# Moving one attention product into the next unit's group, and two output projection chunks to later steps

## The chip, the cores and the metric

The kernel runs on one core of one Trainium2 chip. The metric is the device time of one execution in microseconds (us). Engines: TensorE (PE; its weight loads are PEld), VectorE (DVE), ScalarE (ACT), GpSimd (POOL) and SyncE (SP), which only issues transfers. Each engine works through its own instructions in order and waits on semaphores of the others. TensorE writes to PSUM, eight banks of 128 partitions by 512 floats; VectorE and ScalarE read them.

## The reference

One transformer block on 2048 tokens of width 576: a modulated layer norm, attention with 32 heads of width 18 in four segments of 512 tokens and a memory that goes from segment to segment, an output projection with a residual, a second modulated norm, and a gated MLP of width 4608. The part that matters here:

```python
for s in range(N):
    qs, ks, vs = q[:, :, s], k[:, :, s], v[:, :, s]
    logits = jnp.einsum("bhqd,bhkd->bhqk", qs, ks) * scale + mask
    p = _softmax(logits, axis=-1)
    a_dot = jnp.einsum("bhqk,bhkd->bhqd", p, vs)
    ...
    o = g * a_mem + (1.0 - g) * a_dot
...
return o @ wo
```

The mask subtracts 1e9 where the key index is below the query index, so a query sees its own key and the later ones. All is float32.

## The kernel before

The kernel has three stages. The first (to 244.9 us of the profile) makes the projections and memory states, and already begins the maxima of the first units. The second, from 244.9 to 599.9 us, is the attention, and the third is the rest of the output projection and the MLP. The change touches the second stage only.

**Units and steps.** The attention is cut into 32 units: segment `s` and a group `q` of four heads, `u = 8 s + q`. A loop (L1350 on) runs over `u` and one more round for what is left over, with 11 steps `k` in each unit. The order of the instructions is the order in which this loop calls functions; nothing else schedules them. Each step takes, in this order:

- one piece of `p2_step(u, j)` (L590): the logits of one key block `j` of 128 keys against the queries, transposed (keys on partitions). These are the score matmuls, L601, into one of two banks `s2`, and the exponential on ScalarE, L604, from there to `Pt`. Block 0 takes steps 0 to 3 (one head each, 512 queries), block 1 steps 4 to 7 (384 queries), block 2 steps 8 and 9 (two heads each, 256 queries), block 3 step 10 (four heads, 128 queries). Behind a block GpSimd masks it (L608). `Pt` has one buffer for each block.
- one piece of `p1_step(u + 2, ...)` (L172): the logits of a unit two ahead in the other orientation, only for the row maxima. These are the maximum matmuls, L182, into one of two banks `s1`, and the reduction with the mask on VectorE, L187. Steps 0 to 3 have one reduction of 512 keys each, steps 4 to 7 one of 384, steps 8 and 9 two of 256, step 10 four of 128. The reduction of step `k` empties the bank that the maximum matmul of step `k + 2` writes.
- the events that the table `PAT` (L60) lists for this step. It has four rows: even and odd units of the first half of a segment (`q` below 4), and even and odd units of the second half.

**The events that matter.** `V0` to `V3` (`av_step`, L612) multiply block `j` of `Pt` with the values: four matmuls for four heads, each on 32 columns of the array (L621), which run at the same time and add into one bank `av`. Before, `V0` and `V1` belong to the unit at hand and `V2` and `V3` to the one before. `E` copies `av` with ScalarE (L633), `m` transposes the maxima (L201), `c` and `d` transpose and normalize the result. `M0` to `M3` (`wo_m`, L731) are the four chunks of one half of a 128-token tile of the output projection, of 3, 4, 3 and 4 matmuls, in one bank `w`; `X` (`wo_x`, L736) adds them to the residual on VectorE, which frees the bank, and at every second unit stores the tile (L738). They run in units 9 to 32. `R`, `S`, `T`, `Z`, `z` prepare the projection's left operand (`T` is L715 on VectorE, `z` is L693), `P`, `Q`, `q`, `Y` its weights in units 0 to 5 (`Y` is `wol`, L914, on VectorE); `l`, `p`, `x` are the second norm, `f`, `g`, `h` the memory's feature map (`g` is three ScalarE instructions, L780 to L782), `A` to `D` and `G` the memory's part.

Of the kernel before, what the change touches and what calls it, by code (L numbers as in the profile page):

```python
# [15 lines left out]
P = 128  # L16
S = 2048
D = 576
# [38 lines left out]
NE = 2  # L57
E1 = 3
E2 = 2
PAT = (["", "M0", "V2 V3 m E D", "", "n M1 Q G", "c", "M2 d", "V0 g", "h A0 q M3 R S X", "T Y Z B0", "A1 P V1 z B1 f C"],  # L60
# [3 lines left out]
LNA = 1  # L64
S1B, S2B, XB, WB = 2, 2, 2, 1

# [6 lines left out]
def block(ctx: ExitStack, tc: tile.TileContext, x, wqk, wv, wo, beta, wgu, wd, c, w_mod, out):  # L73
# [8 lines left out]
    def chain(*g):  # L82
        for a in g:
            yield from a
# [113 lines left out]
    def mt_a(u, ps, tag, bufs):  # L198
        mc = mcol.pop(u)[1]
        pmt[u] = ps.tile([P, L], F32, tag=tag, name="pmt", bufs=bufs)  # L200
        nc.tensor.transpose(pmt[u][:32, :P], f32(mc).rearrange("p a b c -> p (a b c)"), ident)  # L201

    def mt_b(u):
        mrow[u] = mr = mwk.tile([32, P], F32, tag="mr", name="mr")
        nc.scalar.copy(mr, pmt.pop(u)[:32, :P])
        put_m(u, u % NB)
# [38 lines left out]
    with ExitStack() as p1:  # L245
# [78 lines left out]
        with ExitStack() as p0:  # L324
# [41 lines left out]
            for b in range(3):  # L366
                n = P if b < 2 else 64
# [89 lines left out]
        def proj(s, t):  # L457
            hh, hl, hr = hT[s]
            pp = ps.tile([P, L], F32, tag="p", name="pp", bufs=3)
            mm14(pp, lambda k: wqkh[:, t, k, :], lambda k: wqkl[:, t, k, :], lambda k: hh[k],  # L460
                 lambda k: hl[k], lambda: hr, True)
            f = pb.tile([P, L], F32, tag="pf", name="pf")
            fh = pb.tile([P, L], F32R, tag="fh", name="fh")
            fl = pb.tile([P, L], F32R, tag="fl", name="fl")
            nc.scalar.copy(fh, pp)
            nc.scalar.copy(f, pp)
            nc.vector.tensor_tensor(fl, f, f32(fh), op=ALU.subtract)
            k0, k1 = 128 * t, min(128 * t + 128, D)
            if k0 < D:
                n = k1 - k0  # L470
                nc.sync.dma_start(kD[s][k0:k1, 0:2, :], f32(fh[:n]).unsqueeze(1).to_broadcast([n, 2, L]))
                nc.sync.dma_start(kD[s][k0:k1, 2, :], f32(fl[:n]))
            q0, q1 = max(128 * t - D, 0), 128 * t + 128 - D
            if q1 > 0:
                n = q1 - q0
                r = P - n
                nc.sync.dma_start(qD[s][q0:q1, 0:3:2, :], f32(fh[r:]).unsqueeze(1).to_broadcast([n, 2, L]))
                nc.sync.dma_start(qD[s][q0:q1, 1, :], f32(fl[r:]))
                if s > 0:
                    nc.sync.dma_start(qF[s][q0:q1, :], f[r:])  # L480
            return f
# [34 lines left out]
        for s in range(NSEG):  # L516
# [5 lines left out]
            g = chain(*gens)  # L522
# [6 lines left out]
            for t in QKORD:  # L529
# [4 lines left out]
                f = proj(s, t)  # L534
# [77 lines left out]
    def av_step(u, j):  # L612
        if u < 0 or u >= NU:
            return
        s, q = units[u]
        if j == 0:
            av[u] = ps.tile([P, L], F32, tag="av", name="av", bufs=1)
        pt = Pt.pop((u, j))
        for h in range(4):
            hh = 4 * q + h  # L620
            nc.tensor.matmul(av[u][32 * h:32 * h + 32, 128 * j:L], lhsT=vq[s][:, j, VW * hh:VW * hh + 32],  # L621
                             rhs=pt[:, h, :L - 128 * j], start=(j == 0), stop=(j == 3))
# [3 lines left out]
    def ev_step(u):  # L626
        if u < 0:
            return
        t = wk.tile([P, L], F32, tag="avs", name="avs")
        if u < NE - 2:  # L630
            nc.vector.tensor_copy(t, av.pop(u))
        else:
            nc.scalar.copy(t, av.pop(u))  # L633
        avs[u] = t

    def comb_a(u):
        if u < 0:
            return
        t = avs[u]
        avs[u] = px = ps.tile([P, 4, P], F32, tag="x", name="px", bufs=XB)  # L640
        for i in range(4):
            nc.tensor.transpose(px[:, i, :], t[:, 128 * i:128 * i + 128], ident)  # L642
# [127 lines left out]
    def phi_q(s, t):  # L770
        r = 64 if t == 0 else 0
        q0 = 0 if t == 0 else 64 + 128 * (t - 1)
        f = wk.tile([P, L], F32, tag="qf", name="qf", bufs=2)
        nc.sync.dma_start(f[r:], qF[s][q0:q0 + P - r, :])
        return f

    def phi_q2(s, t, f):
        r = 64 if t == 0 else 0
        e = wk.tile([P, L], F32, tag="qe", name="qe", bufs=1)
        nc.scalar.activation(e[r:], f[r:], AF.Relu, scale=-1.0)  # L780
        nc.scalar.activation(e[r:], e[r:], AF.Exp, scale=-1.0)
        nc.scalar.activation(f[r:], f[r:], AF.Relu)  # L782
        return e
# [61 lines left out]
    def event(ev, u):  # L845
        n, a = ev[0], ev[1:]
        s, q = divmod(u, 8)
        if n == "V":
            j = int(a)
            av_step(u if j < 2 else u - 1, j)  # L850
        elif n == "E":
            ev_step(u - 1)
        elif n == "m":
            if NE <= u + 1 < NU:
                mt_a(u + 1, ps, "x", XB)
        elif n == "n":
            if NE <= u + 1 < NU:
                mt_b(u + 1)
        elif n == "c":
            comb_a(u - 1)  # L860
        elif n == "d":
            comb_b(u - 1)
        elif n == "f":
            sn, qn = divmod(u + 1, 8)
            if u + 1 < NU and sn < 3 and qn < 5:
                fq[u + 1] = phi_q(sn + 1, qn)
        elif n in "gh" and s < 3 and q < 5:
            if n == "g":
                fq[-2] = phi_q2(s + 1, q, fq[u])
            else:  # L870
                phi_q3(s + 1, q, fq.pop(u), fq[-2])
        elif n in "DG" and u > 0:
            s1, q1 = divmod(u - 1, 8)
            if s1 < 3 and q1 >= 4:
                (num_d if n == "D" else num_e)(s1 + 1, q1 - 4, fq[-3])
        elif n in "ABC" and s < 3 and 4 <= q < 8:
            if n == "A":
                num_a(s + 1, q - 4, int(a))
            elif n == "B":
                num_b(s + 1, q - 4, int(a))  # L880
            else:
                fq[-3] = num_c(s + 1, q - 4)
        elif n in "Zz" and 1 <= s < 4 and q == 0:
            (wo_z if n == "Z" else wo_z2)(s - 1)
        elif n in "RST" and 1 <= s < 4 and q % 2 == 0:
            (wo_r if n == "R" else wo_s if n == "S" else wo_t)(s - 1, q // 2)
        elif n in "MX":
            w = u - 9
            if w >= 0 and w < 24:
                si, h = divmod(w, 2)  # L890
                if n == "M":
                    wo_m(si // 4, si % 4, h, int(a))
                else:
                    wo_x(si // 4, si % 4, h)
        elif n in "lpx":
            w = (u - 9) | 1 if u % 2 == 0 else u - 10
            if 0 <= w < 23:
                if n == "l":
                    ln_a(w // 8, w % 8 // 2)
                elif n == "p":  # L900
                    ln_b()
                else:
                    ln_c()
        elif n == "P" and s == 0 and q < 5:
            fq[-1] = wk.tile([P, D], F32, tag="woraw", name="woraw", bufs=1)
            nc.sync.dma_start(fq[-1], wo[:, q, :])
        elif n in "QqY" and s == 0 and 1 <= q < 6:
            k = q - 1
            if n == "Q":
                nc.gpsimd.tensor_tensor(fq[-1], fq[-1], gaB, op=ALU.mult)  # L910
            elif n == "q":
                nc.scalar.copy(woh[:, k], fq[-1])
            else:
                nc.vector.tensor_tensor(wol[:, k], fq[-1], f32(woh[:, k]), op=ALU.subtract)  # L914
# [212 lines left out]
    O, W, R, RW, DP = {}, {}, {}, {}, {}  # L1127
# [79 lines left out]
    T, SG, AC, AP = {}, {}, {}, {}  # L1207
# [136 lines left out]
    with tc.manual_schedule():  # L1344
# [5 lines left out]
        for u in range(NU + 1):  # L1350
            s, q = divmod(u, 8)
# [3 lines left out]
            for k in range(11):  # L1355
# [4 lines left out]
                if u == 24 and k == 0:  # L1360
                    stage_b()
                for ev in PAT[q // 4 * 2 + u % 2][k].split():
                    event(ev, u)
# [37 lines left out]
        for i in range(4):  # L1401
            for h in range(2):
                for c in range(WC):
                    n = 8 * i + 4 * h + c
# [4 lines left out]
                    if n in SS:  # L1409
                        j = SS.index(n)  # L1410
# [3 lines left out]
                    if n in WW:  # L1414
                        j = WW.index(n)
# [21 lines left out]
        n, nw = 0, PF  # L1437
# [5 lines left out]
        for t in range(2):  # L1443
            for p in range(NPR):
# [16 lines left out]
                for k in range(14):  # L1461
                    z, m = ZM[k]
# [67 lines left out]
                    if prev is not None and is_plain(*prev):  # L1530
# [3 lines left out]
                        if CH0[t][k]:  # L1534
                            f = plain(*prev, chunk)
# [20 lines left out]
                    if is_plain(t, p):  # L1556
                        if k in DK[dl // 2]:
                            j = DK[dl // 2].index(k)
# [74 lines left out]
```

## Time and profile before

| what | us |
|---|---|
| median of three runs | 1890.95 (1889.97 to 1894.65) |
| the profiled execution | 1891.12 |
| its span, first to last instruction | 1889.4 |
| first stage | 0 to 244.9 |
| attention stage | 244.9 to 599.9 |
| last stage | 599.9 to 1889.4 |

The page gives each engine's busy time, the chain that ended last, and groups of instructions by line. A row of the windows gives a stretch, its length, and the busy time and the number of instructions of TensorE, its weight loads, VectorE, ScalarE and GpSimd, then the granted clock, the share of the DMA engines and their rate. A row of the waits says who waited for whom: total us, times, longest. A row of the timeline has start, duration, engine, line, operation, what is written and read, the shape, the number of instructions merged, and in brackets the idle time of the engine before it with the instruction that ended it. A busy TensorE is modelled: the difference of two starts is the better measure of what a matmul costs.

### The profile page before, as it was taken

To read this page: it belongs to the slowest core of one execution; us is meant where nothing else is said; L and a number is where in the kernel's file an instruction comes from. 1 tells how busy PE (TensorE), PEld (TensorE's weight loads), DVE (VectorE), ACT (ScalarE), POOL (GpSimd) and SP (SyncE) were. 2 spreads that over 40 slices of the span, in tenths; PEclk is the share of its full clock that TensorE was granted. 3 is DMA by queue.
4 is the path that set the end of the run, shared out by engine and by line. 5 is a ranking of instruction groups with operands and counts; after the bars stand their busy time and mean duration, and the time that the engine had idled before them with its cause. 6 is when DMAs were issued, how large, how long until landed. Compare 5 with 4: busy or idle time off the path is not lost.

```text
span 1889.4 us, 30685 instructions
## 1 busy us (share of the span) xinstructions
PE 1861.1 (98%) x10927; PEld 1564.1 (83%) x10927; DVE 1495.0 (79%) x3279; ACT 971.8 (51%) x2128; POOL 532.1 (28%) x713
## 2 busy tenths in 40 slices
PE   7999999999999999999999999999999999999999
PEld 5888866777766788888888888888888888888888
DVE  6556368888886888888888988867888888888887
ACT  4433477768676544544544454444454444444442
POOL 2000046555556354455455455300000000000000
PEclk9999999999999999999999999999999999999999
DMA  8767654447555845544554544487233332333331
GB/s 246 261 204 257 218 175 133 145 132 201 168 161 186 293 146 179 182 144 168 169 177 144 191 141 142 162 275 227 79 122 103 121 106 77 125 103 118 102 100 57
DMA packets 179424, 304.31 MB, mean 161 GB/s; under 512 B 26152, under 2 KB 107688, under 8 KB 177352
## 3 DMA queue, kind: packets, MB, share of 16 engines
q1 hardware_dynamic: 150696, 245.29, 41.6%
q10 hardware_dynamic: 28576, 57.07, 8.5%
q8 instruction: 86, 1.41, 0.3%
q14 instruction: 66, 0.54, 0.1%
HBM read 187.98 MB, written 113.77 MB: 160 GB/s over the span
## 4 chain that ended last, share of the span: by engine, by line
PE 91%; DVE 3%; ACT 2%; DMA 1%; POOL 1%; issue 1%; SPq 0%; ACTq 0%; DVEq 0%; POOLq 0%
PE A L1204 24%; PE pd L1325 13%; PE C L1204 12%; PE pd L1308 10%; PE B L1204 6%; PE pp L99 5%; PE s L601 4%; PE s L182 4%; PE av L621 4%; PE pv L99 3%; PE pw L731 3%; DVE junk L187 1%; PE pn L802 1%; PE pm L449 1%; PE px L642 1%
## 5 line engine op out<-in xcount | busy, mean ns | idle before, releaser
L1204 PE MATMUL A<-y,wh 128*128 128x512 f32 x1152 | 407.1, 394 | 2.8 <-ACT tc L1233 2.0
L187 DVE CUSTOM_DVE_ANT_0 junk<-s,tri 128x256 bf16<-128x256 f32 (+3 forms) x512 | 227.9, 487 | 65.9 <-PE s L182 58.8
L1169 DVE TENSOR_TENSOR wl<-O,wh 128x256 fp32r<-128x256 f32 x504 | 258.5, 518 | 2.3 <-ACT wh L1168 1.8
L1204 PEld LDWEIGHTS A<-y,wh 128*128 128x128 f32 x1152 | 217.1, 188 | 47.8 <-ACT tc L1233 2.4
L1204 PE MATMUL A<-y,wl 128*128 128x512 f32 x576 | 227.2, 394 | 0.0
L604 ACT ACTIVATE Pt<-s 128x512 f32<-128x512 f32 (+1 forms) x352 | 186.1, 559 | 53.6 <-PE s L601 48.1
L1313 DVE TENSOR_TENSOR acc<-acc,pd 128x576 f32<-128x576 f32 x216 | 162.4, 752 | 58.6 <-PE pd L1308 51.5
L1159 POOL TENSOR_TENSOR O<-O 128x384 f32<-128x384 f32 x140 | 160.0, 1156 | 164.9 <-DMA O<-in_wgu_dram 72.5
L1204 PE MATMUL C<-y,wh 128*128 128x512 f32 x576 | 202.7, 392 | 1.8 <-DVE cu L1227 1.8
L1168 ACT CAST wh<-O 128x256 fp32r<-128x256 f32 x504 | 197.7, 406 | 1.7 <-issue 0.9
L1325 PE MATMUL pd<-dh,ah 128*128 128x288 f32 x640 | 189.2, 296 | 0.0
L1325 PE MATMUL pd<-dh,al 128*128 128x288 f32 x640 | 189.1, 296 | 0.0
L1325 PE MATMUL pd<-dl,ah 128*128 128x288 f32 x640 | 188.9, 295 | 0.0
L1329 DVE TENSOR_TENSOR acc<-acc,pd 128x576 f32<-128x576 f32 x156 | 116.9, 750 | 89.2 <-PE pd L1325 89.1
L1268 ACT CAST ah<-sg 128x512 fp32r<-128x512 f32 x192 | 119.4, 622 | 81.9 <-DVE sg L1228 81.7
L601 PE MATMUL s<-qs,ks 110*128 110x512 f32 (+2 forms) x384 | 148.3, 403 | 2.9 <-ACT Pt L604 2.4
L1269 DVE TENSOR_TENSOR al<-sg,ah 128x512 fp32r<-128x512 f32 x192 | 135.3, 704 | 9.9 <-ACT ah L1268 9.7
L182 PE MATMUL s<-ks,qs 108*128 108x256 f32 (+3 forms) x512 | 142.0, 329 | 0.9 <-DVE mx L187 0.2
L1308 PE MATMUL pd<-dh,ah 128*128 128x288 f32 x448 | 133.0, 297 | 0.0
L1308 PE MATMUL pd<-dh,al 128*128 128x288 f32 x448 | 132.5, 296 | 0.0
L1308 PE MATMUL pd<-dl,ah 128*128 128x288 f32 x448 | 132.3, 295 | 0.0
L1204 PEld LDWEIGHTS C<-y,wh 128*128 128x128 f32 x576 | 108.3, 188 | 22.3 <-DVE cu L1227 2.2
(361 smaller groups left out, 4385.1 us busy)
## 6 DMA issues: line engine op xcount, KB each, us to landing
O<-in_wgu_dram SPq DMA_DIRECT2D x36, 768.0 KB
oD<-O ACTq DMA_DIRECT2D x36, 512.0 KB
O<-oD SPq DMA_DIRECT2D x36, 512.0 KB
ks<-kD SPq DMA_DIRECT2D x64, 216.0 KB
qs<-qD SPq DMA_DIRECT2D x64, 216.0 KB
O<-in_wgu_dram SPq DMA_DIRECT2D x36, 384.0 KB
rD<-wr ACTq DMA_DIRECT2D x36, 336.0 KB
wr<-rD SPq DMA_DIRECT2D x35, 336.0 KB
```

The costliest lines, as they stand in the source:

```text
L99: nc.tensor.matmul(ps, lhsT=a, rhs=b, start=(k == 0), stop=(k == 13))
L182: nc.tensor.matmul(bank[:, n * (h - h0):n * (h - h0) + n], lhsT=qst[b][0:108, h, 128 * i:128 * i + 128], rhs=kst[b][0:108, h // 2, 0:n], s ...
L187: nc.vector.tensor_tensor_reduce(junk[:, :n], bank[:, n * (h - h0):n * (h - h0) + n], tri[:, L - n:], 1.0, -3e38, op0=ALU.add, op1=ALU.max ...
L601: nc.tensor.matmul(bank[:, n * (g - h):n * (g - h + w)].rearrange("p (a b) -> p a b", a=w), lhsT=kst[u % NB][0:110, g // 2, 128 * j:128 * ...
L604: nc.scalar.activation(pt[:, h:h + per, :n], bank[:, :n * per].rearrange("p (a b) -> p a b", a=per), AF.Exp, scale=SCALE)
L1159: eng.tensor_tensor(o[:, d], o[:, a], o[:, b], op=op)
L1168: nc.scalar.copy(wh, o)
L1169: later.append(lambda: nc.vector.tensor_tensor(wl, o, f32(wh), op=ALU.subtract))
L1204: nc.tensor.matmul(bank, lhsT=a, rhs=b, start=(first and n == 0), stop=(n == 6), skip_group_check=not first)
L1308: nc.tensor.matmul(pd[:, i, :288], lhsT=a[:, tk], rhs=w, start=(k == 0), stop=(k == 2))
L1313: nc.vector.tensor_tensor(o, o, pd[:, :, :288], op=ALU.add)
L1325: nc.tensor.matmul(pd[:, i, :288], lhsT=a[:, tk], rhs=w, start=(k == 0), stop=(k == 5))
```

## The change

`V1` leaves step 10 and stands in front of `V2` and `V3` in the next unit, at step 2 (step 3 in the last row), and `av_step` is told that blocks 1 to 3 belong to the unit before. `M3` with `X` goes to step 9 from step 8 or 6; in the last row `X` stays in step 10 and `M3` comes to step 9 from step 6. In the first two rows `M2` goes from steps 6 and 4 to steps 8 and 6. Only the table and one line differ:

```diff
-PAT = (["", "M0", "V2 V3 m E D", "", "n M1 Q G", "c", "M2 d", "V0 g", "h A0 q M3 R S X", "T Y Z B0", "A1 P V1 z B1 f C"],
-       ["D", "l M0 Q", "V2 V3 m E", "M1", "G p n A0 B0 M2", "", "M3 X A1 q c x d B1", "f", "V0 g", "", "C V1 Y h P"],
-       ["", "M0", "V2 V3 m E", "", "D G M1 c n", "", "Q V0 d g R", "h", "M2 q M3 A0 S B0 X", "Z Y", "P f z V1 A1 T B1 C"],
-       ["", "M0", "l D p G", "V2 V3 m E", "n M1 M2 A0", "", "M3 x c", "B0", "V0 d Q", "A1 g", "q X V1 Y B1 h P C f"])
+PAT = (["", "M0", "V1 V2 V3 m E D", "", "n M1 Q G", "c", "d", "V0 g", "h A0 q M2 R S", "T Y Z B0 M3 X", "A1 P z B1 f C"],
+       ["D", "l M0 Q", "V1 V2 V3 m E", "M1", "G p n A0 B0", "", "M2 A1 q c x d B1", "f", "V0 g", "M3 X", "C Y h P"],
+       ["", "M0", "V1 V2 V3 m E", "", "D G M1 c n", "", "Q V0 d g R", "h", "M2 q A0 S B0", "Z Y M3 X", "P f z A1 T B1 C"],
+       ["", "M0", "l D p G", "V1 V2 V3 m E", "n M1 M2 A0", "", "x c", "B0", "V0 d Q", "A1 g M3", "q X Y B1 h P C f"])
...
         if n == "V":
             j = int(a)
-            av_step(u if j < 2 else u - 1, j)
+            av_step(u - (j > 0), j)
```

## Prediction

> **What bounds the kernel now.** I read the page first, then the busy time by stage, then the waits of the attention stage (244.9 to 599.9 us, the only one that the change touches), then its timeline at the ends of units.
>
> ```profile
> PE 1861.1 (98%) x10927; PEld 1564.1 (83%) x10927; DVE 1495.0 (79%) x3279; ACT 971.8 (51%) x2128; POOL 532.1 (28%) x713
> ...
> PE 91%; DVE 3%; ACT 2%; DMA 1%; POOL 1%; issue 1%; SPq 0%; ACTq 0%; DVEq 0%; POOLq 0%
> ```
>
> ```profile
> core 0: us, PE busy (x) PEld busy (x) DVE busy (x) ACT busy (x) POOL busy (x), PEclk, DMA share, GB/s
> ...
> 334.50:419.50 85.00, 84.95 (x652) 62.81 (x652) 68.92 (x290) 61.66 (x127) 44.48 (x93) 1.00 0.47 141
> ```
>
> ```profile
> DVE junk L187 <- PE s L182: 56.1, 84, 13.2
> ...
> PEld s L601 <- ACT Pt L604: 31.2, 55, 1.1
> ...
> PEld s L182 <- DVE mx L187: 8.0, 28, 0.5
> ```
>
> By the page and its chain it is TensorE, and in the stage (here the units of its second segment) TensorE shows no gap at a granted clock of 1.00. But VectorE is busy for 68.9 of 85.0 us, and the two wait for each other in turn: reductions for maximum matmuls, and 28 times the weight load of a maximum matmul for a reduction. What counts is who leads just where the product leaves and where it arrives. The end of unit 1 and the start of unit 2 (start, duration; idle before it in brackets):
>
> ```profile
> 262.74 0.42 DVE L187 CUSTOM_DVE_ANT_0 junk<-s,tri 128x256 bf16<-128x256 f32 x1 [0.28 <-PE s L182]
> ...
> 263.26 0.85 PE L621 MATMUL av<-Pt,vq 128*32 128x384 f32 x8
> ...
> 264.05 0.50 PE L601 MATMUL s<-qs,ks 110*128 110x512 f32 x1
> 264.06 0.29 DVE L187 CUSTOM_DVE_ANT_0 junk<-s,tri 128x128 bf16<-128x128 f32 x1
> 264.27 0.78 DVE L914 TENSOR_TENSOR wol<-woraw,woh 128x576 fp32r<-128x576 f32 x1
> ...
> 264.98 0.68 DVE L187 CUSTOM_DVE_ANT_0 junk<-s,tri 128x512 bf16<-128x512 f32 x1
> ...
> 265.59 0.68 DVE L187 CUSTOM_DVE_ANT_0 junk<-s,tri 128x512 bf16<-128x512 f32 x1
> 265.72 0.51 PE L182 MATMUL s<-ks,qs 108*128 108x512 f32 x1
> ...
> 266.15 0.86 PE L621 MATMUL av<-Pt,vq 128*32 128x256 f32 x16
> 266.26 0.69 DVE L187 CUSTOM_DVE_ANT_0 junk<-s,tri 128x512 bf16<-128x512 f32 x1
> ...
> 266.94 0.28 PE L201 MATMUL pmt<-ident,mc 128*32 128x128 f32 x1
> ...
> 267.74 0.69 DVE L187 CUSTOM_DVE_ANT_0 junk<-s,tri 128x512 bf16<-128x512 f32 x1 [0.78 <-PE s L182]
> ```
>
> From 262.74 to the end of the reduction of 266.26 VectorE does not pause. The maximum matmul of step 2 (265.72) needs the bank that the reduction of step 0 empties at 264.98 + 0.68 = 265.66. So the product of block 1 (263.26 to 264.05) lies in time that TensorE spends anyway: without it TensorE comes earlier and waits for the same 265.66. In step 2 it is the other way round: behind the products of blocks 2 and 3 VectorE is already out of work (0.78 us idle before 267.74), and nothing covers one more.
>
> **The change part by part.**
>
> *The product out of step 10, 32 times.* It holds TensorE for 264.05 - 263.26 = 0.79 us. How much of that TensorE wins is its lead at the joined group, worked out below: at least 0, at most the 0.79 and what the change of shape costs around it.
>
> *The product into the joined group.* Blocks 2 and 3 together have 256 + 128 = 384 columns, as many as block 1, and also take 0.79 us (266.15 to 266.94). The first block alone, with 512:
>
> ```profile
> 352.82 1.07 PE L621 MATMUL av<-Pt,vq 128*32 128x512 f32 x8
> 353.82 0.50 PE L601 MATMUL s<-qs,ks 110*128 110x512 f32 x1
> ```
>
> takes 1.00. So 128 columns cost 0.21, 384 cost 0.63, and 0.16 of each group is entry and exit, of which the joined group needs one less. I take 0.66 for the product in its new place, a little over the 0.63 since that difference is rounded; the ends are 0.63 and 0.79. On ScalarE the copy of av and the exponentials of the next steps stand behind the longer group, and on VectorE the reduction of step 3: all go later by what is not won back. Block 1's exponentials are then three steps older, and the next writer of their single buffer is step 4, behind the group: no new wait.
>
> *The lead by kind of unit end.* The bound is VectorE's idle time ahead of the new unit's first reduction (first and last of each kind; unit 1 above and unit 28 are the first kind):
>
> ```profile
> 569.53 0.68 DVE L187 CUSTOM_DVE_ANT_0 junk<-s,tri 128x512 bf16<-128x512 f32 x1
> ...
> 347.36 0.69 DVE L187 CUSTOM_DVE_ANT_0 junk<-s,tri 128x512 bf16<-128x512 f32 x1 [0.56 <-POOL Pt L608]
> 556.79 0.69 DVE L187 CUSTOM_DVE_ANT_0 junk<-s,tri 128x512 bf16<-128x512 f32 x1 [0.47 <-PE s L182]
> ...
> 380.90 0.69 DVE L187 CUSTOM_DVE_ANT_0 junk<-s,tri 128x512 bf16<-128x512 f32 x1 [0.47 <-POOL mc L195]
> 498.89 0.69 DVE L187 CUSTOM_DVE_ANT_0 junk<-s,tri 128x512 bf16<-128x512 f32 x1 [0.39 <-PE s L182]
> ...
> 391.98 0.45 DVE L736 TENSOR_TENSOR xr<-pw,xr 128x288 f32<-128x288 f32 x1
> 392.57 0.69 DVE L187 CUSTOM_DVE_ANT_0 junk<-s,tri 128x512 bf16<-128x512 f32 x1
> ...
> 393.47 0.40 PE L182 MATMUL s<-ks,qs 108*128 108x512 f32 x1
> ...
> 449.54 0.69 DVE L187 CUSTOM_DVE_ANT_0 junk<-s,tri 128x512 bf16<-128x512 f32 x1 [0.36 <-POOL mc L192]
> ...
> 315.94 0.69 DVE L187 CUSTOM_DVE_ANT_0 junk<-s,tri 128x512 bf16<-128x512 f32 x1 [1.01 <-PE s L182]
> ```
>
> 1. No pause, or under 0.2 us: the ends of units 1 to 5, 8, 10, 16, 24, 28 and 29, eleven of them. Here wol, ol, the split of the last 64 columns or, in unit 29, the residual sum fills VectorE. I take a lead of 0.07 on average and a loss of 0.59 each: 6.5 us.
> 2. Odd units of the first half of a segment from 9 on, six: 0.47 to 0.56 of idle time, lead 0.5, loss 0.16 each: 1.0 us.
> 3. Units 12, 14, 20, 22: 0.39 to 0.47, lead 0.44, loss 0.22 each: 0.9 us.
> 4. Units 13, 15, 21, 23: after the residual sum (391.98 + 0.45) only 0.14 idle, but the matmul of step 2 comes 393.47 - 393.26 = 0.21 after the reduction that it needs; lead 0.32, loss 0.34 each: 1.4 us.
> 5. Units 18 and 26, between kinds 1 and 2 (449.54: 0.36 idle): lead 0.27, loss 0.39 each: 0.8 us.
> 6. Units 0 and 7, idle like kind 2: 0.3 us together. Unit 6 (1.01 idle before 315.94): TensorE wins the whole 0.79 and a little around it, a gain of 0.2.
> 7. Unit 30, without reductions, is held by its exponentials: 0.3 lost; the last product has nothing behind it but output chunks: 0.2 gained.
>
> Sum: 6.5 + 1.0 + 0.9 + 1.4 + 0.8 + 0.3 - 0.2 + 0.3 - 0.2 = +10.8 us. With lead 0 everywhere it would be 31 x 0.66 = +20.5 us; with the full 0.79 and the saved change of shape everywhere it is rival A's gain.
>
> *The output chunks.* Unit 10 before:
>
> ```profile
> 354.39 0.29 PE L731 MATMUL pw<-wol,oh 128*128 128x288 f32 x1
> ...
> 354.91 0.60 PE L704 MATMUL pto<-ident,o 128*128 128x128 f32 x4
> ...
> 355.28 0.45 DVE L736 TENSOR_TENSOR xr<-pw,xr 128x288 f32<-128x288 f32 x1
> ...
> 357.33 0.28 DVE L187 CUSTOM_DVE_ANT_0 junk<-s,tri 128x128 bf16<-128x128 f32 x1
> ...
> 358.21 0.69 DVE L187 CUSTOM_DVE_ANT_0 junk<-s,tri 128x512 bf16<-128x512 f32 x1
> 358.31 0.50 PE L182 MATMUL s<-ks,qs 108*128 108x512 f32 x1
> ```
>
> The last chunk (four matmuls, 354.91 - 354.39 = 0.52 us) goes to step 9, so step 9 starts 0.52 earlier and step 10 at the old time; the third chunk goes two steps later in the patterns of the first half of a segment. TensorE's sum is zero. But the residual sum (0.45 us of VectorE) follows the last chunk to step 9, out of a place with idle time and in front of the four small reductions of step 10. In unit 10 these start only at 357.33 and end at 358.21, and the maximum matmul of step 1 waits for them until 358.31. The earlier reductions of step 9 (0.5) about pay for the sum (0.45): between -0.1 and +0.1 us for each of the 18 sums that move (the last pattern keeps its place), 1.8 us in all, so I put it at 0. On SyncE the store behind every second sum goes one step later, ahead of the same load as before, and in two units behind one store of yD; nothing waits for it within the unit. The norm that reads the sum runs in the next unit, three steps or more behind the new place, which hides the move; without that cover each move would cost its way, one to three steps of 85.0 / 8 / 11 = 0.97 us. ScalarE and GpSimd issue what they did, in the same order; only TensorE, VectorE and SyncE change theirs.
>
> Sum of all: 1891.1 us for the profiled run (span 1889.4) + 10.8 = 1901.9; the median before is 1890.95, so 1902.
>
> **The rivals.**
>
> A. *Only the saved entry and exit counts; faster.* If ScalarE and VectorE kept up, TensorE would win at the old place 0.79 and the slow first score matmul and lose 0.66:
>
> ```profile
> 357.35 0.50 PE L601 MATMUL s<-qs,ks 110*128 110x512 f32 x1
> 357.69 0.40 PE L182 MATMUL s<-ks,qs 108*128 108x512 f32 x1
> 357.92 0.39 PE L601 MATMUL s<-qs,ks 110*128 110x512 f32 x1
> ```
>
> After the group the score matmul takes 0.34, the next one 0.23. So 0.79 + 0.11 - 0.66 = 0.24 a unit, 31 x 0.24 = 7.4 us: 1884. For it: TensorE 98% busy. Against: 265.72 following 265.66. It decides where the lead exceeds 0.66, which only unit 6 shows. [...]
>
> B. *The lag is paid back; no change.* ScalarE and VectorE stand still during the longer group, but the 31.2 + 8.0 us of weight loads that waited for them might shrink in steps 3 to 9. If a quarter of that vanishes, 10 us, the sum is zero: 1891. For it: those waits. Against: they are waits of the load, which runs ahead; TensorE itself has 0.05 us of gaps in 85.
>
> C. *The moved sums and exponentials eat the leads too; slower still.* Lead 0 at all ends: 1911.6. For it: VectorE's 81% in the stage. Against: 0.39 to 0.56 us of idle time at the ten ends of kinds 2 and 3.
>
> **How the numbers follow.** Forecast 0.67, own range 1897 to 1907 (lead 0.2 more or less at 31 ends is 6 us, partly excluding each other); A 0.15, B 0.10, C 0.08. A measurement tells about 0.3%, 5.7 us. Slower 0.67 + 0.08 = 0.75, same 0.10, faster 0.15. Leaving out A and the outer half of C, the range is 1889 to 1909.
>
> **What would show it.** Right: the joined group about 1.45 us from its first product to the transpose behind it; in kind 1 step 2 still starts with the end of a reduction, and the idle time before the reduction of step 3 grows from 0.78 to about 1.4; VectorE busy as before and the stage 11 us longer, the rest unchanged. Wrong: reductions of step 0 that start over 0.3 us earlier in kind 1, or steps 3 to 9 that become shorter than before by more than the moved chunks.

## The result, and the profile after

The changed kernel takes 1905.56 us (median of 4, 1904.13 to 1906.25), the kernel before 1891.76 us beside it: a ratio of 1.0067, 95% interval 1.0055 to 1.0079. That is 13.8 us slower by the medians and 12.7 by the ratio; the forecast was 1902 us, about 11 us slower, with a range of 1889 to 1909. The profiled run took 1905.54 us, its span is 1903.8.

The page of the changed kernel, its busy times and its chain:

```profile
PE 1864.5 (98%) x10927; PEld 1564.0 (82%) x10927; DVE 1494.4 (78%) x3279; ACT 972.2 (51%) x2128; POOL 531.8 (28%) x713
...
PE 90%; DVE 5%; ACT 2%; POOL 1%; issue 1%; DMA 1%; SPq 0%; DVEq 0%; ACTq 0%; POOLq 0%
```

TensorE is still the bound, but VectorE's share of the chain has gone from 3% to 5%. The busy times by stage, first the kernel before, its attention stage and its last stage:

```profile
244.90:599.80 354.90, 350.33 (x2598) 244.77 (x2596) 287.24 (x1176) 268.74 (x556) 201.10 (x382) 1.00 0.53 153
599.80:1889.40 1289.60, 1279.09 (x6989) 1122.81 (x6987) 1078.95 (x1802) 603.61 (x1390) 305.66 (x273) 1.00 0.46 149
```

and the same two of the changed kernel:

```profile
244.98:614.82 369.84, 355.51 (x2598) 245.43 (x2596) 288.85 (x1176) 268.51 (x556) 201.04 (x382) 1.00 0.51 147
614.82:1903.80 1288.98, 1277.15 (x6988) 1121.92 (x6987) 1076.83 (x1802) 603.96 (x1390) 305.42 (x273) 1.00 0.46 149
```

All of it lies in the attention stage: 369.84 - 354.90 = +14.9 us. TensorE's busy time there grows by 5.2 us and its time without work from 354.90 - 350.33 = 4.6 to 14.3 us. The waits of that stage:

```profile
DVE junk L187 <- PE s L182: 70.6, 87, 13.2
...
PEld s L601 <- ACT Pt L604: 27.9, 62, 1.1
PEld s L182 <- DVE mx L187: 24.4, 61, 1.1
...
PE s L182 <- DVE mx L187: 6.6, 20, 0.8
```

Weight loads of maximum matmuls wait 61 times for a reduction (28 before), and now the matmuls themselves wait too: 20 times, 6.6 us (once, 0.2 us, before). VectorE in its turn waits 70.6 us for maximum matmuls, 14.5 more. Each engine waits for the other, in different steps. The timeline at the end of unit 1, which the prediction shows of before:

```profile
263.93 0.50 PE L601 MATMUL s<-qs,ks 110*128 110x512 f32 x1 [0.48 <-ACT Pt L604]
...
264.39 0.80 DVE L914 TENSOR_TENSOR wol<-woraw,woh 128x576 fp32r<-128x576 f32 x1
...
265.11 0.68 DVE L187 CUSTOM_DVE_ANT_0 junk<-s,tri 128x512 bf16<-128x512 f32 x1
...
265.85 0.51 PE L182 MATMUL s<-ks,qs 108*128 108x512 f32 x1 [0.17 <-DVE mx L187]
...
266.28 1.50 PE L621 MATMUL av<-Pt,vq 128*32 128x384 f32 x24
...
267.72 0.28 PE L201 MATMUL pmt<-ident,mc 128*32 128x128 f32 x1
...
268.51 0.69 DVE L187 CUSTOM_DVE_ANT_0 junk<-s,tri 128x512 bf16<-128x512 f32 x1 [1.42 <-PE s L182]
```

Most of the 0.79 us that left step 10 has become a wait of 0.48 us for an exponential at step 0 and one of 0.17 us for VectorE at step 2: the maximum matmul of 265.85 again follows the end of a reduction, 265.11 + 0.68 = 265.79. The joined group takes 267.72 - 266.28 = 1.44 us, and VectorE then stands idle for 1.42 us.

Another kind of end, that of unit 13, shows where most of the win goes:

```profile
398.46 0.42 PE L601 MATMUL s<-qs,ks 110*128 110x512 f32 x1
...
398.77 0.29 DVE L187 CUSTOM_DVE_ANT_0 junk<-s,tri 128x128 bf16<-128x128 f32 x1
398.98 0.08 DVE L187 DVE_READ_ACCUMULATOR2_ANT mx<- 128x1 f32 x1
398.98 0.46 DVE L736 TENSOR_TENSOR xr<-pw,xr 128x288 f32<-128x288 f32 x1
...
399.12 0.50 PE L182 MATMUL s<-ks,qs 108*128 108x512 f32 x1 [0.24 <-DVE mx L187]
...
399.49 0.19 PEld L731 LDWEIGHTS pw<-woh,oh 128*128 128x128 f32 x1 [0.18 <-DVE xr L736]
```

and the same place in the kernel before:

```profile
391.98 0.08 DVE L187 DVE_READ_ACCUMULATOR2_ANT mx<- 128x1 f32 x1
...
392.37 0.40 PE L601 MATMUL s<-qs,ks 110*128 110x512 f32 x1
...
392.61 0.39 PE L182 MATMUL s<-ks,qs 108*128 108x512 f32 x1
...
392.83 0.30 PE L731 MATMUL pw<-woh,oh 128*128 128x288 f32 x1
```

This is the maximum matmul of step 1, not of step 2. It writes the bank of the four small reductions of step 10, and the last of these is read out at 398.98 + 0.08 = 399.06. Before, the matmul came 392.61 - 392.37 = 0.24 us behind the start of its step and 0.55 us after the last small reduction (391.98 + 0.08 = 392.06); now it comes 0.66 behind the start of the step, because it waits for that reduction. The step grows by 0.67 us: 0.42 lie ahead of this matmul, and the rest behind it, where the next output chunk (L731) waits for the residual sum (L736), which in this pattern still stands behind the small reductions.

The table is worked out from the starts of the score matmuls (one step lasts from the first one of a step to that of the next) in the traces of this study: change of all steps of one number, summed over the 31 ends of units, in us, against the kernel before. The two last columns are the sum of the first four, and all steps 4 to 9. Three rows contain stretches in which TensorE's clock fell to half (last section): the changed kernel one, at the end of unit 2; block 1 alone into the group two, at the ends of units 2 and 5 (2.02 and 2.20 us, where units 1 and 8 cost 0.65 and 0.64); block 1 alone to step 0 one, at the end of unit 2.

| kernel | step 10 | step 0 | step 1 | steps 2, 3 | ends | steps 4 to 9 |
|---|---|---|---|---|---|---|
| changed kernel | -24.5 | +0.9 | +10.7 | +23.6 | +10.8 | +4.0 |
| block 1 alone into the group | -22.0 | +3.5 | +9.4 | +25.0 | +15.9 | -1.3 |
| block 1 alone to step 1 | -20.6 | +3.5 | +29.4 | +5.0 | +17.3 | -1.2 |
| block 1 alone to step 0 | -20.2 | +28.7 | +1.0 | -2.0 | +7.5 | -0.3 |
| blocks 0 and 1 in step 10 | +29.1 | +0.1 | -1.3 | -1.4 | +26.4 | -18.7 |
| chunks alone | +0.5 | +0.1 | -0.8 | -0.6 | -0.8 | +5.4 |
| changed kernel with less in step 10, against the one before with the same cut | -24.0 | +0.7 | +1.5 | +22.5 | +0.7 | +3.2 |

In the changed kernel TensorE wins 24.5 us in steps 10, waits 10.7 of them away in steps 1, and pays 23.6 us in the group's step.

### The profile page after: what moved, and what is told of

Read it like the earlier page. It is cut to its first block, busy times and chain, and to the rows that moved or that the text cites. A ratio compares the mean times of both kernels' runs of the same rounds, so it can differ in the third digit from the quotient of the medians.

```text
span 1903.8 us, 30685 instructions
## 1 busy us (share of the span) xinstructions
PE 1864.5 (98%) x10927; PEld 1564.0 (82%) x10927; DVE 1494.4 (78%) x3279; ACT 972.2 (51%) x2128; POOL 531.8 (28%) x713
## 4 chain that ended last, share of the span: by engine, by line
PE 90%; DVE 5%; ACT 2%; POOL 1%; issue 1%; DMA 1%; SPq 0%; DVEq 0%; ACTq 0%; POOLq 0%
PE A L1204 24%; PE pd L1325 13%; PE C L1204 12%; PE pd L1308 9%; PE B L1204 6%; PE pp L99 5%; PE av L621 4%; PE s L182 4%; PE s L601 3%; PE pv L99 3%; PE pw L731 2%; DVE junk L187 2%; PE pm L449 1%; ACT Pt L604 1%; PE pn L802 1%
```

## The experiments

**1. One part of the change at a time.** First the product of block 1 alone, in all four patterns (one is shown), chunks and sums unmoved:

```
-PAT = (["", "M0", "V2 V3 m E D", ..., "A1 P V1 z B1 f C"],
+PAT = (["", "M0", "V1 V2 V3 m E D", ..., "A1 P z B1 f C"],
...
-            av_step(u if j < 2 else u - 1, j)
+            av_step(u - (j > 0), j)
```

> Kernel before with the product of block 1 moved alone, the output chunks and residual sums left where they were. Theory (VectorE leads at the unit ends and nothing covers the longer group): the leads are those of the kernel before, so 1902 to 1906 us, as the whole change. Rival 1 (the moved residual sums in front of the small reductions are the cause): 1890 to 1893 us.

Measured: 1905.47 us, ratio 1.0072 (1.0057 to 1.0087). The product alone gives the whole difference. Then the other part, chunks and sums as in the change, the product of block 1 in step 10:

```
-       ["D", "l M0 Q", "V2 V3 m E", "M1", "G p n A0 B0 M2", "", "M3 X A1 q c x d B1", "f", "V0 g", "", "C V1 Y h P"],
+       ["D", "l M0 Q", "V2 V3 m E", "M1", "G p n A0 B0", "", "M2 A1 q c x d B1", "f", "V0 g", "M3 X", "C V1 Y h P"],
```

> Kernel before with the output chunks and residual sums moved alone, the product of block 1 left in step 10. Theory: 1889 to 1894 us, no change beyond the 1.8 us that the sums were given. Rival 1 (the moved sums are the cause): 1898 us or more.

Measured: 1896.04 us, ratio 1.0026 (1.0016 to 1.0037), between the two expectations: the chunks do cost, some 5 us by themselves. The two parts do not add up (13.6 + 4.9 = 18.5 us by the ratios, against 12.7 of the change). By the table, part of what the chunks lose in steps 4 to 9 is given back at the ends of units when the product is gone from there: these cost 15.9 us with the product alone and 10.8 in the changed kernel, or some 13 and 9 without the stretches of half clock and a slow subtraction. What makes the difference there was not tested.

**2. Less work for VectorE in step 10.** The four small reductions of step 10 of the attention units are replaced by one copy of four columns, in the kernel before and in the changed one; the maxima of the first 128 queries are left out.

```
+            if i == 0 and u >= NE:
+                nc.vector.tensor_copy(mx[:, :, 0:1], mx[:, :, 1:2])
-            for h in range(h0, h0 + per):
+            for h in range(h0, h0 + per if i or u < NE else h0):
```

> Kernel before without the four reductions of step 10 in units of the attention stage; a copy of four columns takes their place, so the maxima of the first 128 queries of a segment are those of the second 128. VectorE loses about 0.75 us a unit end (four times 0.21, less the copy). Theory: TensorE already has the product of block 1 there to fill the time, so only the short stalls at steps 1 and 2 go: 1886 to 1891 us. Rival 2 (the length of the group and the late copy of av on ScalarE are the cause, VectorE is not): 1891 us.

> The changed kernel without the same reductions (same copy, same part left out). Theory: VectorE's chain at the unit end is 0.75 us shorter, TensorE reaches the joined group up to 0.95 us earlier, and the change costs nothing any more or gains: 1884 to 1893 us, within 3 us of the kernel before without these reductions or faster. Rival 2 (the group itself and ScalarE behind it): still 11 to 14 us over the kernel before without these reductions, 1899 us or more.

Measured: 1891.59 us for the kernel before with the cut, ratio 0.9994 (0.9985 to 1.0004), and 1896.13 us for the changed one with it, 1.0023 (1.0013 to 1.0032). Neither hits the theory's number: the kernel before gains nothing, as rival 2 had it, where the theory allowed 1891 at most; the changed one stays 4.5 us above it, where the theory allowed 3 and rival 2 wanted 11 to 14. What speaks for the theory is the difference between the two kernels. The same 14.3 us of VectorE's work are worth nothing in the kernel before and 9.4 us in the changed one. The busy times of the stage, kernel before with the cut:

```profile
247.70:602.20 354.50, 349.05 (x2598) 244.76 (x2596) 272.94 (x966) 268.57 (x556) 200.80 (x382) 1.00 0.53 153
```

and the waits for reductions in the changed kernel with it (lines stand two lower there):

```profile
PEld s L182 <- DVE mx L189: 8.3, 26, 0.8
...
PE s L182 <- DVE mx L189: 1.5, 4, 0.5
```

The waits that had grown to 24.4 and 6.6 us are back at 8.3 and 1.5, and step 1 costs 1.5 us in place of 10.7. Sorted by steps, 27 of the 61 weight loads that wait in the changed kernel, and 13 of the 20 matmuls, stand in steps 1 (14 and 6 in steps 2); with the cut none does in steps 1 (8 weight loads in steps 2). So the small reductions of step 10 are the work behind which TensorE waits in step 1. At the ends of units 12 to 15 and 20 to 23 this pair wins 0.28 to 0.35 us each: here TensorE leads, and the saved entry and exit of a group shows, as rival A had it (0.24). Of the 4.5 us that remain, 3.2 lie in steps 4 to 9, with the chunks.

**3. The product in front of the wait or behind it.** The prediction had the wait at the maximum matmul of step 2. Then a place in step 1 should be as good as step 10:

```
+PAT = (["", "V1 M0", "V2 V3 m E D", ...
+       ["D", "V1 l M0 Q", "V2 V3 m E", ...
+       ["", "V1 M0", "V2 V3 m E", ...
+       ["", "M0", "V1 l D p G", "V2 V3 m E", ...
```

> The product of block 1 alone moved into the next unit, but one step ahead of the group (step 1, in the last pattern step 2), so as a group of its own; output chunks where they were. Theory (VectorE leads up to the maximum matmul of step 2, TensorE behind it): in step 1 the 0.79 us still lie ahead of that wait, so nothing is lost and, with as many groups as before, nothing won: 1889 to 1894 us. Rival (what costs is that the product enters the new unit at all, 0.6 us at most ends, wherever it stands there): 1900 to 1907 us.

Measured: 1907.82 us, ratio 1.0081 (1.0065 to 1.0096). The theory in this form falls; the rival's range ended at 1907, 0.8 us below. The end of unit 13 in its trace:

```profile
399.52 0.50 PE L182 MATMUL s<-ks,qs 108*128 108x512 f32 x1 [0.23 <-DVE mx L187]
...
399.95 0.85 PE L621 MATMUL av<-Pt,vq 128*32 128x384 f32 x8
```

TensorE has waited in step 1 before it comes to the product. So the decisive place had to be one step earlier, and the product went to step 0:

```
+PAT = (["V1", "M0", "V2 V3 m E D", ...
+       ["V1 D", "l M0 Q", "V2 V3 m E", ...
```

> The product of block 1 alone at step 0 of the next unit, behind that step's score and maximum matmuls and ahead of those of step 1; chunks where they were. With the product in step 1 the time came to 1907.8 us, and its trace shows the waits of TensorE already ahead of it: against the kernel before, the 31 steps 10 won only 20.6 of 31 x 0.88 = 27.3 us, the steps 0 lost 3.5 and the steps 1 lost 29.4 us. New theory (TensorE waits in step 1, for the four small reductions of step 10; what stands behind that wait is lost, what stands ahead is not): only the losses up to step 0 remain, 6.7 + 3.5 = 10.2 us at most, less the waits of step 1 that the product then covers: 1894 to 1902 us. Rival (the place does not matter, a product taken out of step 10 is lost wherever the next unit takes it): 1905 to 1909 us.

Measured: 1897.38 us, ratio 1.0026 (1.0016 to 1.0037), inside the new theory's range and below the rival's. One step's place (two in the last pattern), with the same number of groups, is worth 10.4 us. The same end, and three waits of TensorE in the whole stage:

```profile
395.87 0.85 PE L621 MATMUL av<-Pt,vq 128*32 128x384 f32 x8
...
396.08 0.29 DVE L187 CUSTOM_DVE_ANT_0 junk<-s,tri 128x128 bf16<-128x128 f32 x1
...
396.99 0.39 PE L182 MATMUL s<-ks,qs 108*128 108x512 f32 x1
```

```profile
PEld s L601 <- ACT Pt L604: 39.3, 66, 1.1
...
PE s L601 <- ACT Pt L604: 5.8, 14, 1.0
PE s L182 <- DVE mx L187: 1.3, 3, 0.7
```

The last small reduction ends at 396.37 under the product, and the matmul of step 1 comes at 396.99 without a wait. What is left of the loss, 5.3 us, lies at step 10: step 0 pays 28.7 us, 0.93 at each end, about the price of a group, but step 10 wins only 20.2. The score matmul that ends step 10, the first of the next unit, waits 4.1 us for exponentials (0.2 in the kernel before). The weight loads wait more too (39.3 us in place of 31.2), but 16.7 us of that fall to the score matmul just behind the product, where the load waits while TensorE is at work. That these waits are all of the rest is not shown.

**4. One group fewer, but ahead of the wait.** The product of block 0 goes to step 10, beside that of block 1; nothing else moves.

```
-... "V0 g", "h A0 q M3 R S X", "T Y Z B0", "A1 P V1 z B1 f C"],
+... "g", "h A0 q M3 R S X", "T Y Z B0", "A1 P V0 V1 z B1 f C"],
```

> The product of block 0 moved from steps 6 to 8 to step 10, joined there with that of block 1; the rest as before. One group fewer per unit, as in the change, but ahead of the wait for VectorE. Theory 1 (the saved entry and exit of about 0.24 us a unit is won where TensorE leads, and steps 6 to 8 win the whole product): 1884 to 1888 us. Theory 2 (a step without a product lasts as long as its two exponentials and its reduction, so the old place is not won; and at the ends where VectorE and TensorE are level, 0.63 us more before the first maximum matmul of the next unit delays VectorE): 1895 to 1910 us.

Measured: 1900.73 us, ratio 1.0044 (1.0031 to 1.0058), in theory 2's range. By the table step 10 grows by 29.1 us, 0.94 at each end, and steps 4 to 9 win only 18.7, under 0.6 us a unit for a product that takes 1.00 in a group of its own. But theory 2's reason for that is only half right: steps 6 to 8, the old places, win 27.1 us, 0.85 a unit, and step 9 gives 8.7 of them back. There 13 weight loads of maximum matmuls now wait 6.4 us for reductions, and none did before. The saved entry and exit does not show in the time here either.

**5. The chunks, taken apart.** First M2 of the second pattern alone, from step 4 to step 6:

```
-... "G p n A0 B0 M2", "", "M3 X A1 q c x d B1", ...
+... "G p n A0 B0", "", "M2 M3 X A1 q c x d B1", ...
```

> One part of the moved chunks alone: in the second pattern the chunk M2 goes from step 4 to step 6, in front of M3, which stays; six units (9, 11, 17, 19, 25, 27). Theory (of its 0.52 us step 4 wins only 0.40, and step 5 grows by 0.27, as its score matmul waits for an exponential of 0.49 us): +0.39 us in each unit, 1893 to 1895 us with 1891.5 for the kernel before. Rival (the residual sum that moves to step 9 is what costs, not M2): 1891 to 1892 us, no change.

Then the last chunk and the sum alone, to step 9 in three patterns:

```
-... "M3 X A1 q c x d B1", "f", "V0 g", "", ...
+... "A1 q c x d B1", "f", "V0 g", "M3 X", ...
```

> The other part of the moved chunks alone: the last chunk M3 with the residual sum X in step 9 in the first three patterns, all M2 left where they were. Theory (the loss of the moved chunks is that of M2 in the second pattern, 1.9 us by itself; a chunk that goes from step 6 or 8 to step 9 leaves steps that still last as long as before less its own time): 1891 to 1893.5 us with 1892 for the kernel before. Rival (the residual sum ahead of the small reductions of step 10 costs up to 0.1 us each, and both parts add up to the 4.5 us of all moved chunks): 1894 to 1896 us.

Measured: 1894.05 us, ratio 1.0011 (1.0002 to 1.0020), for M2; 1892.07 us, ratio 1.0003 (0.9994 to 1.0012), for M3 and the sum. So the sum ahead of the small reductions costs nothing that can be measured (2.3 us at most by the interval), as the prediction had it, and M2 costs some 2 us. In unit 9 of the kernel with M2 moved, steps 4 to 6 start at 341.50, 341.86 and 342.48:

```profile
341.50 0.34 PE L601 MATMUL s<-qs,ks 110*128 110x384 f32 x1
...
341.86 0.34 PE L601 MATMUL s<-qs,ks 110*128 110x384 f32 x1
341.94 0.49 ACT L604 ACTIVATE Pt<-s 128x384 f32<-128x384 f32 x1 [0.33 <-PE s L601]
...
342.47 0.98 ACT L604 ACTIVATE Pt<-s 128x384 f32<-128x384 f32 x2
342.48 0.19 PEld L601 LDWEIGHTS s<-qs,ks 110*128 110x128 f32 x1 [0.37 <-ACT Pt L604]
```

and in the kernel before at 340.04, 340.80 and 341.16:

```profile
340.04 0.34 PE L601 MATMUL s<-qs,ks 110*128 110x384 f32 x1
...
340.80 0.34 PE L601 MATMUL s<-qs,ks 110*128 110x384 f32 x1
...
341.16 0.34 PE L601 MATMUL s<-qs,ks 110*128 110x384 f32 x1
```

Step 4 shrinks from 0.76 to 0.36 us, the whole time of M2's three matmuls, but step 5, without work beside its two matmuls, grows from 0.36 to 0.62: the score matmul of step 6 needs the bank that the exponential of 341.94 empties at 341.94 + 0.49 = 342.43. Two such steps in a row would be shorter than ScalarE's work for them. Step 6, M2's new place, grows by 0.52 us, from 1.24 to 1.76. All the chunks together (1896.04) come to 4.9 us by the ratio and these two runs to 2.1 + 0.6, but each of the three intervals is over 3 us wide; in the traces, from the first step to the last, the two add up: 2.9 + 1.4 us against 4.6. A further cost is therefore not shown.

None of these versions beats the kernel before.

## Why the prediction was right, and where it was off

- *The product out of step 10.* Right in kind: VectorE's reductions bound what TensorE wins. The experiments with fewer reductions (9.4 of the 13.8 us gone) and with the product in front of the wait (10.4 us better than one step later) show it. Wrong in place: the prediction worked the leads out at the maximum matmul of step 2; at most ends the wait is at that of step 1, behind the small reductions of step 10 (10.7 us), which the prediction showed in the kernel before (358.31) only in its part on the chunks. Where VectorE makes no pause, as in kind 1, the lead is the same at either. In kind 4 it is not: the margin at step 1 was 0.55 us, not the 0.21 of step 2, and the chunk that waits for the residual sum took the difference, so this kind's good number is partly luck. A third place was not in the prediction: at the ends of units 1 to 4 the score matmul of step 0 or its weight load waits for an exponential first, as at 263.93, and step 10 wins only 0.24 to 0.56 us there; at the end of unit 26 such a wait is 0.44 us.
- *The product into the group.* Right: 0.59 to 0.71 us more in the group's step at 24 of the 31 ends (0.66 was taken), 1.44 us to the transpose (1.45), 1.42 us of idle time on VectorE (1.4).
- *The lead by kind.* The sum over the 31 ends is +10.8 us in the two traces, as predicted, but by errors that cancel. Per end, measured against taken: kind 1 0.66 against 0.59, of which the end of unit 2 with 1.88 holds 1.2 us of a lower clock and that of unit 3 half a microsecond of a slow subtraction (both below); kind 2 0.19 against 0.16; kind 3 0.08 against 0.22; kind 4 0.31 against 0.34; kind 5 0.38 against 0.39; units 0 and 7 0.04 against 0.15; unit 6 -0.29 against -0.2; unit 30 0.31 against 0.3. Without the two disturbances the ends cost about 9. The range, 1889 to 1909, took in even no change, so that the time lies inside says little; what speaks for the mechanism is the experiments.
- *The output chunks put at 0.* This is the term that failed: steps 4 to 9 lost 4.0 us in the changed kernel. The prediction said that TensorE's sum is zero, and looked for the cost at the residual sum only. The runs showed the sum to be free within the interval, and the cost of M2 to lie around its two places: step 4 gave back the 0.40 us of its three matmuls, but step 5 took 0.26 more, and step 6 paid 0.52 for it. That the chunks cost 4.9 us alone, and none on top of the product alone (1905.56 against 1905.47), says that the two terms share time, or that the difference is lost in the scatter; a split of the 13.8 us into a part for each is therefore only as good as the trace in which it is read.
- *The stage 11 us longer and VectorE busy as before.* 14.9 us, and 288.85 for 287.24 us.
- *The rivals.* A's saving is real, 0.28 to 0.35 us an end, where TensorE leads: at unit 6, and at eight ends once the small reductions were taken out. What this saving is made of no run separates, and it was not what set the time. B's payback came to little: waits of the score matmuls' weight loads for exponentials fell from 31.2 to 27.9 us, and those of the maximum matmuls' for reductions grew from 8.0 to 24.4. C would have been 1911.6.

## What to carry to other kernels

Work that TensorE does ahead of a wait for another engine may cost nothing there, and up to its whole length elsewhere; before moving it, follow the other engines' queues from its old place to the first wait, in every bank, also of the small instructions, and put it in front of that wait if it must move. Do the same for the place that it leaves: here one step shrank to 0.36 us, but two in a row could not become shorter than their two exponentials of 0.49 us. To test such a reading, put the work one step earlier and one step later; here that step was worth 10.4 us, while the saved entry and exit of a group was worth 0.3 us an end at best.

## What the runs showed of the hardware

*TensorE's clock falls to half for about 3.4 us, now and then.* In the changed kernel's trace this hits the group of unit 3, from 275.83 to 279.24 us by the means 0.66 and 0.70 of the second and last rows, 0.50 between them (the last three columns are the granted clock, the DMA share and the rate):

```profile
275.30:275.70 0.40, 0.23 (x1) 0.00 (x0) 0.40 (x7) 0.40 (x2) 0.40 (x2) 1.00 0.00 0
275.70:276.10 0.40, 0.29 (x1) 0.29 (x2) 0.40 (x3) 0.40 (x1) 0.40 (x2) 0.66 0.45 46
...
278.00:279.00 1.00, 1.00 (x12) 0.40 (x8) 0.20 (x2) 0.00 (x0) 1.00 (x1) 0.50 0.61 190
279.00:279.40 0.40, 0.40 (x12) 0.20 (x7) 0.00 (x0) 0.00 (x0) 0.27 (x1) 0.70 0.46 128
```

The end of unit 2, in which this group lies, costs 1.88 us, where those of units 1 and 5 cost 0.66 and 0.64. The trace of the kernel before has such a stretch in the last stage instead, at 651 us, and that of the product moved alone has two in this stage, at 277 and 311 us. They come back at nearly the same places: of the eleven traces, three have one near 25 us, three one between 274 and 278, and seven one between 649 and 667. Ahead of the one shown TensorE has short gaps, of 0.47, 0.16 and 0.28 us from 273.0 to 275.8; ahead of that at 651 us it has one of 1.75. No run here shows that such gaps are the cause. Nor is it shown that the new waits make such stretches more frequent, since the mean granted clock of every run lies between 0.996 and 1.000, with the kernel before as with the others. They are part of the scatter of single runs: in the 24 runs of the kernel before that stood beside experiments 1 and 2, all with a clock of 0.997 took 1893.4 us or more, all with 1.000 at most 1891.6. But they are not all of it: of the seven runs with the product in step 0 the fastest (1896.29) had 0.997.

*One subtraction on VectorE took 1.24 us in place of 0.75.* At the end of unit 3, first the kernel before:

```profile
284.02 0.75 DVE L914 TENSOR_TENSOR wol<-woraw,woh 128x576 fp32r<-128x576 f32 x1
```

```profile
286.70 1.24 DVE L914 TENSOR_TENSOR wol<-woraw,woh 128x576 fp32r<-128x576 f32 x1
```

GpSimd's work beside it, again the kernel before first:

```profile
283.45 1.82 POOL L608 TENSOR_SCALAR_AFFINE_SELECT Pt<-Pt 128x512 f32<-128x512 f32 x2 [2.04 <-ACT Pt L604]
```

```profile
286.11 1.23 POOL L608 TENSOR_SCALAR_AFFINE_SELECT Pt<-Pt 128x512 f32<-128x512 f32 x2 [2.04 <-ACT Pt L604]
287.30 0.70 POOL L192 TENSOR_SCALAR mc<-mx 128x16 fp32r<-128x16 f32 x1
```

In the kernel before the pair of selects takes 0.59 us more and the subtraction its 0.75; in the changed kernel it is the other way round, and the small GpSimd operation that follows, 0.20 us elsewhere, takes 0.70. The second select and the subtraction start almost together, 0.02 us apart at most in these two traces: in the kernel before the subtraction is first and the select takes 1.23 us, in the changed kernel the select is first and takes 0.64. In both the one that starts later is the longer; no run isolated the cause. At this end the subtraction took 1.24 us in six of the eleven traces, among them those with the chunks alone moved (at 284.99) and with the product in step 0, and 0.75 in the kernel before, in that with the product alone in the group and in both with less in step 10, where the select took about 1.2 (with the product alone although it started first, by less than 0.01 us). So it is no mark of the change.
